# Turning the attention weights: from TensorE transposes to VectorE blocks and 16 transfers, with a new order of loads and conversions

## The chip, the cores and the metric

The kernel runs on one core of a Trainium2 chip. The metric is device time in microseconds (us), the median of several executions. A ratio in this text is the mean time of one kernel's fast runs over the mean time of the other kernel's fast runs of the same rounds, so it is not quite the ratio of the medians that are quoted.

Engine names in the profile: PE is TensorE, PEld its weight loads, DVE is VectorE, ACT is ScalarE, POOL is GpSimd, SPq is the DMA queue that SyncE issues. SBUF and PSUM are the core's two on-chip memories: in this kernel TensorE's results land in PSUM, and q, k, v and the weights e stand in SBUF. The granted clock is the share of full clock that TensorE got, by the profile's records. Each fp32 product of this kernel leaves two records on PE (x8 for the four products of a unit's scores), a transpose one; the counts below are of records.

## The reference

Eight batch rows go through attention with a threshold and then through a token and channel mixer; all is float32.

```python
# q, k, v: (8 rows, 8 heads, 576 queries/keys, 64)
scores = q @ k.T / 8
scores = where(scores >= max(scores) - tau, scores, -1e9)
attn   = exp(scores - max) / (sum + 1e-9)
x      = (attn @ v), heads side by side            # (8, 576, 512)
h  = relu(x.T @ w_tok1) @ w_tok2 ;  u = x + h.T    # 256 hidden tokens
out = u + relu(u @ w_ch1) @ w_ch2                  # 1536 hidden channels
```

The weights of the mixer arrive as float64 and are converted on the chip, in 31 pieces.

## The kernel before

A **unit** is 128 queries of a pair of heads; there are 18 units in a row, 144 in all. `t` is the unit's place (0 to 8) in a group of two pairs. While row b's attention runs, the mixer of row b-1 is cut into small steps, which `fill` puts between the attention's instructions. Row 0 has nothing to fill with.

```python
def load_pair(n, eng=nc.sync):        # 14 transfers a pair
    ...                               # lq, lk: 10 transfers in blocks of 32 columns
    vl = vlast[n % VL]
    for h in range(2):
        nc.sync.dma_start(out=lv[:, h], in_=v[b, 2*p+h, 0:MAIN, :]...)
        nc.sync.dma_start(out=vl[D*h:D*h+D, D*h:D*h+D], in_=v[b, 2*p+h, MAIN:S, :])   # v's last 64 rows

def scores(u):      # TensorE: q k^T into two PSUM tiles sc; then, for each head:
    nc.vector.tensor_reduce(out=mx..., in_=sc..., op=ALU.max)
    nc.gpsimd.tensor_scalar(out=bias..., in0=mx..., ...)
def weigh(u):       # ScalarE: e from sc (frees sc), then exp with the row sum
    nc.scalar.activation(out=eh, in_=sc[h]..., func=AF.Prelu, bias=bias...)
    nc.scalar.activation(out=eh, in_=eh, func=AF.Exp, ...)
def norm(u):        # VectorE 1/sum, GpSimd e *= 1/sum
def turn(u, third): # three 128x128 TensorE transposes into PSUM, then a copy to eT
    for c in range(3):
        nc.tensor.transpose(out=ps[:, c, :], in_=e[:, k0:k0+P], identity=ident)
    on = nc.scalar.copy if third == 1 else nc.vector.tensor_copy
    on(out=eT[...], in_=ps)
def values(...):    # TensorE: v^T eT, then a ScalarE copy to xT

for u in range(len(units) + LAG + 1):
    w = u - LAG
    if back and b_now: turn(w, 0); turn(w, 1)
    scores(u); norm(u - 1)
    for i in range(2 if b_now else 0, 3): turn(w, i)
    fill(0.4); weigh(u); fill(0.3)
    ...values of the units turned one step ago...
    fill(0.3)                          # in row 0 instead: weight(2), two steps of a conversion
    if t == 1: load_pair(n + 2)
    if t == 4: load_pair(n + 3)
    ...                                # t == 2, 7: VectorE turns the next q and k
```

Of the kernel before, what the change touches and what calls it, by code (L numbers as in the profile page):

```python
# [17 lines left out]
P = 128  # L18
# [3 lines left out]
def kernel(  # L22
# [11 lines left out]
):  # L34

# [53 lines left out]
    def load_pair(n, eng=nc.sync):  # L89


        b, p = pairs[n]
        lq = ld.tile([P, S // 32, 32], F32, tag="lq", name=f"lq_{n}")
        lk = ld.tile([P, S // 32, 32], F32, tag="lk", name=f"lk_{n}")
        lv = ld.tile([P, 2, NI, D], F32, tag="lv", bufs=4, name=f"lv_{n}")
        nl = LAST // 32
        for h in range(2):
            for c in range(2):
                r = slice(64 * h + 32 * c, 64 * h + 32 * c + 32)
                cols = slice(32 * c, 32 * c + 32)  # L100
                sq = q[b, 2 * p + h, :, cols].rearrange("(n t) d -> t n d", t=32)
                sk = k[b, 2 * p + h, :, cols].rearrange("(n t) d -> t n d", t=32)
                eng.dma_start(out=lq[r], in_=sq)
                if h == 0:
                    eng.dma_start(out=lk[r], in_=sk)
                else:
                    eng.dma_start(out=lk[r, nl:], in_=sk[:, : MAIN // 32])
                    eng.dma_start(out=lk[r, :nl], in_=sk[:, MAIN // 32 :])
        vl = vlast[n % VL]
        for h in range(2):  # L110
            nc.sync.dma_start(out=lv[:, h], in_=v[b, 2 * p + h, 0:MAIN, :].rearrange("(c p) d -> p c d", p=P))
            nc.sync.dma_start(out=vl[D * h : D * h + D, D * h : D * h + D], in_=v[b, 2 * p + h, MAIN:S, :])
        loaded[n] = (lq, lk, lv, vl)

    ident = const.tile([P, P], F32, name="ident")
# [3 lines left out]
    load_pair(0)  # L119
    load_pair(1, nc.scalar)  # L120
# [14 lines left out]
    abs_at = scratch[:, 2 * WMAX * NRAW + 2 * WMAX : 2 * WMAX * NRAW + 3 * WMAX].bitcast(F32)  # L135
# [7 lines left out]
    def f64_to_f32(dst, raw, rows, n):  # L143
# [10 lines left out]
        h = abs_at[0:rows, 0:n]  # L154
        turn_of[0] += 1
        af = a.bitcast(F32)
        nc.scalar.activation(out=lo.bitcast(I32), in_=lo, func=AF.Copy, scale=2.0**-29)
        yield nc.vector.tensor_scalar(
            out=a, in0=hi, scalar1=3, scalar2=0x3FFFFFFF, op0=ALU.logical_shift_left, op1=ALU.bitwise_and
        )  # L160
        nc.scalar.activation(out=h, in_=hi.bitcast(F32), func=AF.Abs)
# [3 lines left out]
        nc.vector.scalar_tensor_tensor(out=af, in0=h, scalar=2.0**-15, in1=af, op0=ALU.is_ge, op1=ALU.mult)  # L165
# [31 lines left out]
    def weight_ops():  # L197
        for i, (dst, src) in enumerate(pieces):
            raw, rows, n = raws.pop(i)
            if src.dtype == I64:  # L200
                for _ in f64_to_f32(dst, raw.bitcast(U32).rearrange("p (n w) -> p n w", w=2), rows, n):
                    yield
            else:
                nc.gpsimd.tensor_copy(out=dst, in_=like(raw, dst))
# [5 lines left out]
    done = 0  # L210

    def weight(n):

        nonlocal done
        for _ in range(n):
            if next(wops, wops) is wops:
                return
            done += 1

    for i in range(NRAW):  # L220
        load_piece(i)

# [9 lines left out]
    good = const.tile([P, 1], F32, name="good")  # L232
    ntau = const.tile([P, 1], F32, name="ntau")
    toff = const.tile([P, 1], F32, name="toff")
    tlow = const.tile([P, 1], F32, name="tlow")
    nc.vector.tensor_scalar(out=good, in0=tau_sb, scalar1=0.0, scalar2=None, op0=ALU.is_ge)
    nc.vector.tensor_scalar(out=tlow, in0=good, scalar1=1.0, scalar2=3.0e38, op0=ALU.subtract, op1=ALU.mult)
    nc.vector.tensor_scalar(out=ntau, in0=tau_sb, scalar1=0.0, scalar2=FAR, op0=ALU.max, op1=ALU.min)
    nc.vector.tensor_scalar(out=toff, in0=ntau, scalar1=-1.0 / SCALE, scalar2=None, op0=ALU.mult)
# [300 lines left out]
```

## Time and profile before

| | before |
|---|---|
| median | 1547.4 us (1547.0 to 1550.2; three runs. With a fourth, taken beside the changed kernel, 1547.2 us) |
| TensorE busy, share of the chain that ended last | 1472.7 us, 86% |
| mean granted TensorE clock | 0.99 |
| rows 0 and 1, from first scores to first scores | 101 and 188 us |
| rows 3 to 6, the same | 171, 187, 174, 190 us |

The busy share alone says little, since records of pipelined products overlap. The chain that ended last says more: where it runs through TensorE, only less work on TensorE shortens the kernel. Waits name who released whom. Few waits of TensorE over 1 us stand in the trace before (21, 40 us in all); the longest are at the start and in rows 0 and 1. The two kinds of wait that matter below are small here (who waited for whom; us in total, times, longest):

```profile
PE sc L271 <- ACT e L286: 6.8, 5, 2.0
...
PE c L393 <- ACT g L394: 2.8, 8, 0.7
```

### The profile page before, as it was taken

To read this page: it belongs to the slowest core of one execution; us is meant where nothing else is said; L and a number is where in the kernel's file an instruction comes from. 1 tells how busy PE (TensorE), PEld (TensorE's weight loads), DVE (VectorE), ACT (ScalarE), POOL (GpSimd) and SP (SyncE) were. 2 spreads that over 40 slices of the span, in tenths; PEclk is the share of its full clock that TensorE was granted. 3 is DMA by queue.
4 is the path that set the end of the run, shared out by engine and by line. 5 is a ranking of instruction groups with operands and counts; after the bars stand their busy time and mean duration, and the time that the engine had idled before them with its cause. 6 is when DMAs were issued, how large, how long until landed. Compare 5 with 4: busy or idle time off the path is not lost.

```text
span 1545.4 us, 20795 instructions
## 1 busy us (share of the span) xinstructions
PE 1472.7 (95%) x8000; PEld 951.0 (62%) x8000; DVE 542.4 (35%) x1127; ACT 674.3 (44%) x1463; POOL 335.7 (22%) x617
## 2 busy tenths in 40 slices
PE   5778799999999999999999999999999989999999
PEld 3444566647576567565756576566667556765665
DVE  4676763334333333323323342333322333201000
ACT  4776554445455344454434354444434444510110
POOL 2553542222222112212112222221111222200000
PEclk9998999999999999999999999999999999999999
DMA  6253413021111100200210201110201100000000
GB/s 115 68 113 91 132 56 60 8 53 24 31 31 31 31 14 18 47 14 7 54 35 3 43 19 31 31 31 1 60 8 31 31 8 7 1 14 7 7 14 21
DMA packets 206179, 54.05 MB, mean 35 GB/s; under 512 B 192704, under 2 KB 198848, under 8 KB 206080
## 3 DMA queue, kind: packets, MB, share of 16 engines
q1 hardware_dynamic: 201168, 52.13, 15.3%
q10 hardware_dynamic: 4912, 0.59, 0.4%
q8 instruction: 63, 1.03, 0.3%
q14 instruction: 36, 0.29, 0.1%
HBM read 43.25 MB, written 9.44 MB: 34 GB/s over the span
## 4 chain that ended last, share of the span: by engine, by line
PE 86%; ACT 6%; DVE 3%; DMA 2%; SPq 1%; POOL 1%; issue 1%; ACTq 0%; DVEq 0%
PE c L408 24%; PE c L393 22%; PE sc L271 10%; PE tr L321 10%; PE pv L338 7%; PE t L366 5%; PE t L372 3%; PE pv L335 3%; ACT e L289 2%; ACT e L286 2%; PE c L404 1%; PE tx L357 1%; DVE mx L276 1%; DMA lk<-in_k_dram 1%; ACT g L394 0%
## 5 line engine op out<-in xcount | busy, mean ns | idle before, releaser
L393 PE MATMUL c<-xT,wc 128*128 128x256 f32 (+1 forms) x1920 | 403.5, 362 | 4.3 <-ACT g L394 2.8
L408 PE MATMUL c<-wc,g 128*128 128x512 f32 x864 | 387.2, 593 | 0.0
L393 PEld LDWEIGHTS c<-xT,wc 128*128 128x128 f32 x1920 | 333.5, 191 | 59.9 <-ACT g L394 12.5
L323 DVE COPY eT<-tr 128x384 f32<-128x384 f32 x256 | 138.8, 546 | 437.3 <-PE tr L321 437.3
L277 POOL TENSOR_SCALAR bias<-mx,toff 128x1 f32<-128x1 f32 x288 | 76.7, 267 | 954.6 <-DVE mx L276 898.2
L408 PEld LDWEIGHTS c<-wc,g 128*128 128x128 f32 x864 | 157.5, 190 | 165.4 <-issue 164.3
L276 DVE TENSOR_REDUCE mx<-sc 128x1 f32<-128x576 f32 x288 | 204.6, 751 | 143.3 <-PE sc L271 143.2
L394 ACT ACTIVATE g<-c 128x256 f32<-128x256 f32 (+1 forms) x240 | 85.2, 363 | 383.8 <-PE c L393 383.8
L286 ACT ACTIVATE e<-sc,bias 128x576 f32<-128x576 f32 x288 | 199.1, 740 | 112.2 <-POOL bias L277 112.2
L289 ACT ACTIVATE e<-e,ntau,good 128x576 f32<-128x576 f32 x288 | 246.7, 864 | 0.0
L321 PE MATMUL tr<-ident,e 128*128 128x128 f32 x1296 | 210.0, 287 | 32.3 <-ACT eT L323 11.7
L321 PEld LDWEIGHTS tr<-ident,e 128*128 128x128 f32 x1296 | 146.2, 143 | 139.0 <-issue 90.8
L299 POOL TENSOR_SCALAR e<-e,rr 128x576 f32<-128x576 f32 x288 | 218.2, 770 | 19.0 <-DVE rr L296 3.6
L271 PE MATMUL sc<-kT,qT 64*128 64x288 f32 (+1 forms) x1280 | 193.1, 443 | 20.1 <-DVE kT L254 12.9
L271 PEld LDWEIGHTS sc<-kT,qT 64*128 64x128 f32 (+1 forms) x1280 | 103.6, 182 | 68.0 <-issue 20.3
L338 PE MATMUL pv<-eT,lv 128*64 128x256 f32 x1024 | 123.7, 384 | 0.0
L323 ACT COPY eT<-tr 128x384 f32<-128x384 f32 x128 | 61.1, 478 | 137.0 <-PE tr L321 136.7
L413 DVE COPY o<-c 128x512 f32<-128x512 f32 x36 | 24.9, 692 | 214.6 <-PE c L408 214.6
L338 PEld LDWEIGHTS pv<-eT,lv 128*64 128x64 f32 x1024 | 74.9, 139 | 38.6 <-issue 2.6
L372 PE MATMUL t<-w,a 128*128 128x288 f32 x256 | 73.1, 413 | 3.1 <-DVE xT L376 3.1
L366 PE MATMUL t<-x,w 128*128 128x512 f32 (+1 forms) x160 | 75.5, 610 | 0.0
L343 ACT COPY xT<-pv 128x256 f32<-128x256 f32 (+1 forms) x96 | 29.6, 320 | 102.2 <-PE pv L338 102.2
(43 smaller groups left out, 657.5 us busy)
## 6 DMA issues: line engine op xcount, KB each, us to landing
scratch<-in_moe_w_ch_dram SPq DMA_DIRECT2D x24, 512.0 KB, 3.6
out_dram<-o SPq DMA_DIRECT2D x36, 256.0 KB, 2.1
lq<-in_q_dram SPq DMA_DIRECT2D x124, 72.0 KB, 2.6
lv<-in_v_dram SPq DMA_DIRECT2D x64, 128.0 KB, 2.4
lk<-in_k_dram SPq DMA_DIRECT2D x62, 72.0 KB, 2.7
lk<-in_k_dram SPq DMA_DIRECT2D x62, 64.0 KB, 2.4
scratch<-in_moe_w_tok_dram SPq DMA_DIRECT2D x4, 288.0 KB, 3.0
vl<-in_v_dram SPq DMA_DIRECT2D x64, 16.0 KB, 2.1
```

The costliest lines, as they stand in the source:

```text
L271: nc.tensor.matmul(sc[h][rows, f, 0:HS], lhsT=qT[r, cols], rhs=kT[r, HS * f : HS * f + HS], start=True, stop=True)
L276: nc.vector.tensor_reduce(out=mx[:, c], in_=sc[h][:, :, 0:HS], axis=AX.XY, op=ALU.max)
L286: nc.scalar.activation(out=eh, in_=sc[h][:, :, 0:HS], func=AF.Prelu, bias=bias[:, h : h + 1], scale=SCALE, alpha=STEEP)
L289: nc.scalar.activation(out=eh, in_=eh, func=AF.Exp, bias=ntau, scale=good, accum_out=rs[:, h : h + 1])
L299: nc.gpsimd.tensor_scalar(out=eh, in0=eh, scalar1=rr[:, h : h + 1], scalar2=1.0, op0=ALU.mult, op1=ALU.mult)
L321: nc.tensor.transpose(out=ps[:, c, :], in_=e[:, k0 : k0 + P], identity=ident)
L323: on(out=eT[:, 3 * third : 3 * third + 3, c0 : c0 + P], in_=ps)
L338: nc.tensor.matmul(ps[D * h : D * h + D, 0:N], lhsT=lv[:, h, c, :], rhs=eT[:, (NI + 1) * h + c, cols], start=False, stop=(c == NI - 1), sk ...
L366: nc.tensor.matmul(ps, lhsT=w1[0:M, t, P * m : P * m + P], rhs=s["x"][0:M, t, :], start=(t == 0), stop=(t == NT - 1))
L372: nc.tensor.matmul(ps, lhsT=s["a"][:, m, P * c : P * c + P], rhs=w2[:, m, HS * f : HS * f + HS], start=(m == 0), stop=(m == NTK - 1))
L393: nc.tensor.matmul(ps, lhsT=wc1[:, j, c, :], rhs=uT[:, c, GR * i : GR * i + n], start=(c == 0), stop=(c == NCC - 1))
L408: nc.tensor.matmul(flat, lhsT=s["g"][:, j, P * t : P * t + P], rhs=wc2[:, j, :], start=False, stop=(j == NJ - 1), skip_group_check=True)
```

## The change

Its intent: take the transposes of e off TensorE, the bound engine. From row 1 on, VectorE turns e in 32x32 blocks inside SBUF, and 16 transfers per two units move the blocks to where a full transpose would have them. Keys are kept in natural order, so q and k need 8 loads and v one. The 64 rows of v that stand in two tiles are copied to `vl` by GpSimd. Conversions go at a steady pace.

```diff
-    def load_pair(n, eng=nc.sync):
+    def load_qk(n):                   # 8 transfers
+    def load_v(n):
+        lv = ld.tile([P, NK, D], F32, tag="lv", bufs=4, name=f"lv_{n}")
+        nc.sync.dma_start(out=lv, in_=v[b]...)
         vl = vlast[n % VL]
         for h in range(2):
-            nc.sync.dma_start(out=lv[:, h], in_=...)
-            nc.sync.dma_start(out=vl[D * h : D * h + D, D * h : D * h + D], in_=...)
+            r = slice(D * h, D * h + D)
+            nc.gpsimd.tensor_copy(out=vl[r, r], in_=lv[r, NI, :])
 ...
+    def turn_blocks(u):
+        key, place, n = group_of(u)
+        e = st.pop(u)
+        T = Ts[key][:, 0 : NK * n * P]
+        nc.vector.transpose(out=T.rearrange(...)[:, :, :, place, :], in_=e.rearrange("p (c a x) -> p c a x", c=NK, a=4))
+        if place == n - 1:
+            w = NK * n * 32
+            for a in range(4):
+                for i in range(4):
+                    nc.sync.dma_start(out=eTs[key][32*a : 32*a+32, w*i : w*i+w], in_=T[32*i : 32*i+32, w*a : w*a+w])
 ... (conversion: |hi| on ScalarE becomes hi*hi on GpSimd)
-        if back and b_now:
-            turn(w, 0)
-            turn(w, 1)
         if on:
             scores(u)
 ...
+            if in_blocks(key[0]):
+                turn_blocks(w)        # its products with v come two units later
+            else:
+                for i in range(3):
+                    turn(w, i)
 ...
+        weight(1 if b_now == 0 else 3)    # and weight(2) ahead of weigh(u)
         if on:
             if t == 1 and n + 2 < len(pairs):
-                load_pair(n + 2)
+                load_qk(n + 2)
+                load_v(n + 2)
```

More of the change, by code (lines that the diff above doesn't have):

```diff
@@ L87 @@
     vlast = [const.tile([P, P], F32, name=f"vl{i}") for i in range(VL)]
-    def load_pair(n, eng=nc.sync):
+    def load_qk(n):
         b, p = pairs[n]
-        lq = ld.tile([P, S // 32, 32], F32, tag="lq", name=f"lq_{n}")
-        lk = ld.tile([P, S // 32, 32], F32, tag="lk", name=f"lk_{n}")
-        lv = ld.tile([P, 2, NI, D], F32, tag="lv", bufs=4, name=f"lv_{n}")
-        nl = LAST // 32
-        for h in range(2):
-            for c in range(2):
-                r = slice(64 * h + 32 * c, 64 * h + 32 * c + 32)
-                cols = slice(32 * c, 32 * c + 32)
-                sq = q[b, 2 * p + h, :, cols].rearrange("(n t) d -> t n d", t=32)
-                sk = k[b, 2 * p + h, :, cols].rearrange("(n t) d -> t n d", t=32)
-                eng.dma_start(out=lq[r], in_=sq)
-                if h == 0:
-                    eng.dma_start(out=lk[r], in_=sk)
-                else:
-                    eng.dma_start(out=lk[r, nl:], in_=sk[:, : MAIN // 32])
-                    eng.dma_start(out=lk[r, :nl], in_=sk[:, MAIN // 32 :])
+        tiles = []
+        for src, tag in ((q, "lq"), (k, "lk")):
+            t = ld.tile([P, S // 32, 32], F32, tag=tag, name=f"{tag}_{n}")
+            for h in range(2):
+                for c in range(2):
+                    r = slice(64 * h + 32 * c, 64 * h + 32 * c + 32)
+                    nc.sync.dma_start(
+                        out=t[r], in_=src[b, 2 * p + h, :, 32 * c : 32 * c + 32].rearrange("(n t) d -> t n d", t=32)
+                    )
+            tiles.append(t)
+        loaded[n] = tiles
+    def load_v(n):
+        b, p = pairs[n]
+        lv = ld.tile([P, NK, D], F32, tag="lv", bufs=4, name=f"lv_{n}")
+        nc.sync.dma_start(out=lv, in_=v[b].rearrange("h s d -> (h s) d")[2 * S * p : 2 * S * p + 2 * S, :].rearrange("(c p) d -> p c d", p=P))
         vl = vlast[n % VL]
         for h in range(2):
-            nc.sync.dma_start(out=lv[:, h], in_=v[b, 2 * p + h, 0:MAIN, :].rearrange("(c p) d -> p c d", p=P))
-            nc.sync.dma_start(out=vl[D * h : D * h + D, D * h : D * h + D], in_=v[b, 2 * p + h, MAIN:S, :])
-        loaded[n] = (lq, lk, lv, vl)
+            r = slice(D * h, D * h + D)
+            nc.gpsimd.tensor_copy(out=vl[r, r], in_=lv[r, NI, :])
+        vals[n] = lv, vl
+    vals = {}
     ident = const.tile([P, P], F32, name="ident")
@@ L118 @@
         nc.gpsimd.memset(t, 0.0)
-    load_pair(0)
-    load_pair(1, nc.scalar)
+    load_qk(0)
     w1 = const.tile([P, NT, DTOK], F32, name="w1")
@@ L134 @@
     a_at = [scratch[:, 2 * WMAX * NRAW + WMAX * i : 2 * WMAX * NRAW + WMAX * (i + 1)] for i in range(2)]
-    abs_at = scratch[:, 2 * WMAX * NRAW + 2 * WMAX : 2 * WMAX * NRAW + 3 * WMAX].bitcast(F32)
+    sq_at = scratch[:, 2 * WMAX * NRAW + 2 * WMAX : 2 * WMAX * NRAW + 3 * WMAX].bitcast(F32)
     turn_of = [0]
@@ L153, in f64_to_f32 @@
         a = a_at[turn_of[0] % 2][0:rows, 0:n]
-        h = abs_at[0:rows, 0:n]
+        h2 = sq_at[0:rows, 0:n]
         turn_of[0] += 1
@@ L157, in f64_to_f32 @@
         nc.scalar.activation(out=lo.bitcast(I32), in_=lo, func=AF.Copy, scale=2.0**-29)
+        nc.gpsimd.tensor_tensor(out=h2, in0=hi.bitcast(F32), in1=hi.bitcast(F32), op=ALU.mult)
         yield nc.vector.tensor_scalar(
@@ L160, in f64_to_f32 @@
         )
-        nc.scalar.activation(out=h, in_=hi.bitcast(F32), func=AF.Abs)
         yield nc.vector.scalar_tensor_tensor(
@@ L164, in f64_to_f32 @@
         )
-        nc.vector.scalar_tensor_tensor(out=af, in0=h, scalar=2.0**-15, in1=af, op0=ALU.is_ge, op1=ALU.mult)
+        nc.vector.scalar_tensor_tensor(out=af, in0=h2, scalar=2.0**-30, in1=af, op0=ALU.is_ge, op1=ALU.mult)
         nc.gpsimd.tensor_tensor(
@@ L203, in weight_ops @@
             else:
+                yield
+                yield
                 nc.gpsimd.tensor_copy(out=dst, in_=like(raw, dst))
@@ L209 @@
     wops = weight_ops()
-    done = 0
+    steps_done = 0
     def weight(n):
-        nonlocal done
+        nonlocal steps_done
         for _ in range(n):
@@ L217, in weight, with need @@
                 return
-            done += 1
-    for i in range(NRAW):
+            steps_done += 1
+    def need(i):
+        weight(3 * i + 3 - steps_done)
+    load_piece(0)
+    load_qk(1)
+    load_v(0)
+    for i in range(1, NRAW):
         load_piece(i)
+    load_v(1)
     FAR = 104.0
     STEEP = 3.0e38
-    good = const.tile([P, 1], F32, name="good")
+    tlow = const.tile([P, 1], F32, name="tlow")
+    toff = const.tile([P, 1], F32, name="toff")
     ntau = const.tile([P, 1], F32, name="ntau")
-    toff = const.tile([P, 1], F32, name="toff")
-    tlow = const.tile([P, 1], F32, name="tlow")
-    nc.vector.tensor_scalar(out=good, in0=tau_sb, scalar1=0.0, scalar2=None, op0=ALU.is_ge)
-    nc.vector.tensor_scalar(out=tlow, in0=good, scalar1=1.0, scalar2=3.0e38, op0=ALU.subtract, op1=ALU.mult)
-    nc.vector.tensor_scalar(out=ntau, in0=tau_sb, scalar1=0.0, scalar2=FAR, op0=ALU.max, op1=ALU.min)
-    nc.vector.tensor_scalar(out=toff, in0=ntau, scalar1=-1.0 / SCALE, scalar2=None, op0=ALU.mult)
+    nc.vector.tensor_scalar(out=tlow, in0=tau_sb, scalar1=0.0, scalar2=-3.0e38, op0=ALU.is_lt, op1=ALU.mult)
+    nc.vector.tensor_scalar(out=toff, in0=tau_sb, scalar1=0.0, scalar2=FAR, op0=ALU.max, op1=ALU.min)
+    nc.vector.tensor_scalar(out=toff, in0=toff, scalar1=-1.0 / SCALE, scalar2=None, op0=ALU.mult)
     nc.vector.tensor_add(out=toff, in0=toff, in1=tlow)
-    nc.vector.tensor_scalar(out=ntau, in0=ntau, scalar1=-1.0, scalar2=None, op0=ALU.mult)
+    nc.vector.tensor_scalar(out=ntau, in0=toff, scalar1=SCALE, scalar2=None, op0=ALU.mult)
     heads = {}
@@ L247, with in_blocks @@
     eTs = {}
+    Ts = {}
+    def in_blocks(b):
+        return b > 0
     def prep(n):
-        lq, lk, lv, vl = loaded.pop(n)
+        lq, lk = loaded.pop(n)
         made = []
@@ L255, in prep @@
             made.append(sb)
-        heads[n] = made + [lv, vl]
+        heads[n] = made
     def scores(u):
@@ L267, in scores @@
             for n, cols, rows in parts:
-                qT, kT = heads[n][:2]
+                qT, kT = heads[n]
                 for h in range(2):
@@ L282, in weigh @@
         rs = small.tile([P, 2], F32, tag="rs", name=f"rs_{u}")
-        e = work.tile([P, 2 * S], F32, tag="e", bufs=4, name=f"e_{u}")
+        e = work.tile([P, 2 * S], F32, tag="e", bufs=3, name=f"e_{u}")
         for h in range(2):
@@ L288, in weigh @@
             eh = e[:, S * h : S * h + S]
-            nc.scalar.activation(out=eh, in_=eh, func=AF.Exp, bias=ntau, scale=good, accum_out=rs[:, h : h + 1])
+            nc.scalar.activation(out=eh, in_=eh, func=AF.Exp, bias=ntau, accum_out=rs[:, h : h + 1])
         st[u] = e, rs
@@ L300, in norm, with group_of @@
         st[u] = e
+    def group_of(u):
+        b, p0, t = units[u]
+        if t == SHARED:
+            return (b, p0, "s"), 0, 1
+        i, c = divmod(t - (t > SHARED), NI)
+        return (b, p0 + i, c // 2), c % 2, 2
     def turn(u, third):
-        b, p0, t = units[u]
+        key, place, n = group_of(u)
         e = st[u]
-        if t == SHARED:
-            key, c0 = (b, p0, "s"), 0
-        else:
-            i, c = divmod(t - (t > SHARED), NI)
-            key, c0 = (b, p0 + i, c // 2), P * (c % 2)
-        if third == 0 and c0 == 0:
-            if t == SHARED:
-                eTs[key] = work.tile([P, NK, P], F32, tag="eTs", bufs=1, name=f"eTs_{u}")
-            else:
-                eTs[key] = work.tile([P, NK, 2 * P], F32, tag="eT", name=f"eT_{u}")
+        if third == 0 and place == 0:
+            eTs[key] = work.tile([P, NK * 2 * P], F32, tag="eT", name=f"eT_{u}")
         if third == 2:
             st.pop(u)
-        eT = eTs[key]
+        eT = eTs[key][:, 0 : NK * n * P].rearrange("p (c x) -> p c x", c=NK)
         ps = ps_tr.tile([P, MAIN], F32, tag="tr", name=f"tr{third}_{u}")[:, 0 : 3 * P].rearrange("p (c x) -> p c x", c=3)
@@ L322, in turn @@
         on = nc.scalar.copy if third == 1 else nc.vector.tensor_copy
-        on(out=eT[:, 3 * third : 3 * third + 3, c0 : c0 + P], in_=ps)
-    def values(b, p, eT, cols, tok):
-        n = b * NP + p
-        lv, vl = heads[n][2:]
+        on(out=eT[:, 3 * third : 3 * third + 3, P * place : P * place + P], in_=ps)
+    def turn_blocks(u):
+        key, place, n = group_of(u)
+        e = st.pop(u)
+        if place == 0:
+            Ts[key] = work.tile([P, NK * 2 * P], F32, tag="T", name=f"T_{u}")
+        T = Ts[key][:, 0 : NK * n * P]
+        nc.vector.transpose(
+            out=T.rearrange("p (a c n x) -> p c a n x", a=4, c=NK, n=n)[:, :, :, place, :],
+            in_=e.rearrange("p (c a x) -> p c a x", c=NK, a=4),
+        )
+        if place == n - 1:
+            del Ts[key]
+            eTs[key] = work.tile([P, NK * 2 * P], F32, tag="eT", name=f"eT_{u}")
+            w = NK * n * 32
+            for a in range(4):
+                for i in range(4):
+                    nc.sync.dma_start(
+                        out=eTs[key][32 * a : 32 * a + 32, w * i : w * i + w], in_=T[32 * i : 32 * i + 32, w * a : w * a + w]
+                    )
@@ L329, in values @@
+    def values(b, p, c):
+        lv, vl = vals[b * NP + p]
         if b not in xTs:
             xTs[b] = xTs[b + 1] = work.tile([P, NP, 2 * S], F32, tag="xT", name=f"xT_{b}")
-        N = cols.stop - cols.start
-        ps = ps_tr.tile([P, MAIN], F32, tag="tr", name=f"pv_{n}_{tok}")
+        key = (b, p - p % 2, c) if c == "s" else (b, p, c)
+        n, N, tok = (1, LAST, MAIN) if c == "s" else (2, 2 * P, 2 * P * c)
+        first = LAST * (p % 2) if c == "s" else 0
+        eT = eTs[key] if c == "s" else eTs.pop(key)
+        if in_blocks(b):
+            eT = eT[:, 0 : NK * n * P].rearrange("p (i c x) -> p c i x", i=4, c=NK)
+            eT = eT[:, :, first // 32 : first // 32 + N // (32 * n), :]
+        else:
+            eT = eT[:, 0 : NK * n * P].rearrange("p (c x) -> p c x", c=NK)[:, :, first : first + N]
+        ps = ps_tr.tile([P, MAIN], F32, tag="tr", name=f"pv_{b}_{p}_{c}")[:, 0:N]
+        to = ps.rearrange("p (i x) -> p i x", x=32 * n) if in_blocks(b) else ps
@@ L333, in values @@
         for h in range(2):
             r = slice(D * h, D * h + D)
-            nc.tensor.matmul(ps[r, 0:N], lhsT=vl[:, r], rhs=eT[:, NI, cols], start=True, stop=False, skip_group_check=True)
+            nc.tensor.matmul(to[r], lhsT=vl[:, r], rhs=eT[:, NI], start=True, stop=False, skip_group_check=True)
         for c in range(NI):
             for h in range(2):
-                nc.tensor.matmul(
-                    ps[D * h : D * h + D, 0:N], lhsT=lv[:, h, c, :], rhs=eT[:, (NI + 1) * h + c, cols],
-                    start=False, stop=(c == NI - 1), skip_group_check=True,
-                )
@@ L342, in values @@
-        t0 = S * (b % 2) + tok
-        nc.scalar.copy(out=xTs[b][:, p, t0 : t0 + N], in_=ps[:, 0:N])
+                r = slice(D * h, D * h + D)
+                j = (NI + 1) * h + c
+                nc.tensor.matmul(to[r], lhsT=lv[:, j, :], rhs=eT[:, j], start=False, stop=(c == NI - 1), skip_group_check=True)
+        x = xTs[b][:, p, S * (b % 2) + tok : S * (b % 2) + tok + N]
+        if in_blocks(b) and n == 2:
+            x = x.rearrange("p (n i x) -> p i n x", n=n, x=32)
+            ps = ps.rearrange("p (i n x) -> p i n x", n=n, x=32)
@@ L346, in token_mlp @@
+        nc.scalar.copy(out=x, in_=ps)
     def token_mlp(b):
@@ L360, in tok1 @@
         def tok1(m):
+            need(2)
             if m == 0:
@@ L369, in tok2 @@
         def tok2(c, f):
+            need(6)
             ps = ps_mm.tile([P, HS], F32, tag="mm", name=f"t2_{b}_{c}_{f}")
@@ L388, in ch1 @@
         def ch1(j):
+            need(7 + j)
             if j == 0:
@@ L396, in ch2 @@
         def ch2(t, part):
+            need(7 + NJ + 3 * part + 2)
             t0 = GR * i + P * t
@@ L434, in fill @@
             step()
-            if b_now <= 1:
-                weight(2)
         if not todo:
@@ L452 @@
     prep(0)
-    due = []
+    due = deque()
     b_now = 0
     LAG = 2
-    for u in range(len(units) + LAG + 1):
+    for u in range(len(units) + LAG + 4):
         on = u < len(units)
@@ L462 @@
         back = 0 <= w < len(units)
-        ready, due = due, []
-        if back and b_now:
-            turn(w, 0)
-            turn(w, 1)
         if on:
@@ L471 @@
         if back:
-            for i in range(2 if b_now else 0, 3):
-                turn(w, i)
+            key, place, many = group_of(w)
+            if in_blocks(key[0]):
+                turn_blocks(w)
+            else:
+                for i in range(3):
+                    turn(w, i)
+            if place == many - 1:
+                b, p, c = key
+                when = u + (2 if in_blocks(b) else 1)
+                due += [(when, b, p + i, c) for i in range(2 if c == "s" else 1)]
         if b_now:
             fill(0.4)
+        weight(2)
         if on:
@@ L479 @@
             fill(0.3)
-        if back:
-            b, pq, tq = units[w]
-            if tq == SHARED:
-                due += [(b, pq + i, "s") for i in range(2)]
-            else:
-                i, c = divmod(tq - (tq > SHARED), NI)
-                if c % 2 == 1:
-                    due.append((b, pq + i, c // 2))
-        for b, p, c in ready:
-            if c == "s":
-                i = p % 2
-                values(b, p, eTs[b, p - i, c], slice(64 * i, 64 * i + 64), MAIN)
-            else:
-                values(b, p, eTs.pop((b, p, c)), slice(0, 2 * P), 2 * P * c)
-                if c == 1 and p == NP - 1:
-                    push(b)
+        while due and due[0][0] <= u:
+            _, b, p, c = due.popleft()
+            values(b, p, c)
+            if p == NP - 1 and c == 1:
+                push(b)
         if b_now:
             fill(0.3)
-        else:
-            weight(2)
+        weight(1 if b_now == 0 else 3)
         if on:
             if t == 1 and n + 2 < len(pairs):
-                load_pair(n + 2)
+                load_qk(n + 2)
+                load_v(n + 2)
             if t == 2:
@@ L505 @@
             if t == 4 and n + 3 < len(pairs):
-                load_pair(n + 3)
+                load_qk(n + 3)
+                load_v(n + 3)
             if t == 7 and n + 2 < len(pairs):
```

## The prediction

> **What bounds the kernel now.** I read the page first: engine shares, the slices and the chain that ended last.
>
> ```profile
> PE 1472.7 (95%) x8000; PEld 951.0 (62%) x8000; DVE 542.4 (35%) x1127; ACT 674.3 (44%) x1463; POOL 335.7 (22%) x617
> ...
> PE   5778799999999999999999999999999989999999
> ...
> PE 86%; ACT 6%; DVE 3%; DMA 2%; SPq 1%; POOL 1%; issue 1%; ACTq 0%; DVEq 0%
> PE c L408 24%; PE c L393 22%; PE sc L271 10%; PE tr L321 10%; PE pv L338 7%; PE t L366 5%; PE t L372 3%; PE pv L335 3%; ACT e L289 2%; ACT e L286 2%; PE c L404 1%; PE tx L357 1%; DVE mx L276 1%; DMA lk<-in_k_dram 1%; ACT g L394 0%
> ```
>
> TensorE bounds it. From slice 8 on (about 300 us) it stands at 9 in nearly every slice, and it carries 86% of the chain. Only the first 7 slices, 270 us, have slack: row 0 (no MLP to fill with) and row 1 (weights still converting). The part that the change attacks is "PE tr L321", 10% of the chain: the transposes of e.
>
> Second, the groups (line, engine, operation, tiles, shape, count, busy us and mean ns, idle before) for what each operation costs.
>
> ```profile
> L321 PE MATMUL tr<-ident,e 128*128 128x128 f32 x1296 | 210.0, 287 | 32.3 <-ACT eT L323 11.7 <-ACT xT L343 7.1 <-ACT eTs L323 5.2
> L323 DVE COPY eT<-tr 128x384 f32<-128x384 f32 x256 | 138.8, 546 | 437.3 <-PE tr L321 437.3
> L254 DVE STREAM_TRANSPOSE qT<-lq 128x576 f32<-128x576 f32 x32 | 24.6, 769 | 6.1 <-DMA lk<-in_k_dram 6.1
> ```
>
> Third, the timeline of a steady unit, since 287 ns is a modelled record with pipelining in it; starts are what count.
>
> ```profile
> 606.14 0.82 PE L321 MATMUL tr<-ident,e 128*128 128x128 f32 x6
> ...
> 606.89 1.24 PE L271 MATMUL sc<-kT,qT 64*128 64x288 f32 x8
> ...
> 608.06 0.55 PE L321 MATMUL tr<-ident,e 128*128 128x128 f32 x3
> 608.23 1.42 DVE L276 TENSOR_REDUCE mx<-sc 128x1 f32<-128x576 f32 x2 [1.00 <-PE sc L271]
> ...
> 608.45 0.81 PE L393 MATMUL c<-xT,wc 128*128 128x256 f32 x3
> ```
>
> Six transposes occupy TensorE from 606.14 to 606.89 (0.75 us) and three from 608.06 to 608.45 (0.39 us): 1.14 us per unit of 128 queries. Check: 10% of 1545 us over 144 units is 1.07 us.
>
> Fourth, the timeline of the DMA issues on the SyncE queue, because the change adds many.
>
> ```profile
> 1101.36 0.42 SPq L103 DMA_DIRECT2D lq<-in_q_dram  x1
> 1101.83 0.58 SPq L105 DMA_DIRECT2D lk<-in_k_dram  x1
> ...
> 1102.45 0.50 SPq L103 DMA_DIRECT2D lq<-in_q_dram  x1
> 1102.99 0.50 SPq L105 DMA_DIRECT2D lk<-in_k_dram  x1
> ```
>
> Back to back, one issue takes 0.54 us of that queue (1102.45 to 1102.99), whatever its size: the 16 KB loads of vl in the same stretch come at the same pace.
>
> **What the Trainium skill says.** (1) "VectorE: DVE Perf Modes", The three transpose paths: VectorE's transpose does independent 32x32 blocks into SBUF, TensorE's a full 128x128 into PSUM, so the latter needs an evacuation. The trace agrees: 144x3 evacuations (line 323) stand beside the transposes. (2) "TensorE: Matmul & The Clock Gate", Engine queue depths (under Part 1): VectorE, ScalarE and GpSimd are strict FIFO; only TensorE can pull weight loads ahead. The trace's order on these engines is the program's; one instruction that waits holds up all behind it. (3) "DMA: Bandwidth & Descriptors", Issuing engines are not separate DMA queues: the sequencer's time to start a DMA "is usually small relative to the DMA itself". Here it is not: a packet of 2304 B in this trace took 93 ns (median), a transfer of 32 rows is two packets on each of 16 DMA engines, so 0.2 us of engine time against 0.54 us of issue.
>
> **The change part by part.**
>
> *Transposes off TensorE.* Rows 1 to 7 are 126 units: 126 x 1.14 = 144 us of TensorE, all on the path. With them go their waits: between 302 and 1400 us TensorE waited 9 us for PSUM slots of tr (ScalarE's xT and x copies, VectorE's eT copies). Together -153.
>
> *VectorE.* It loses two evacuations per unit (2 x 0.546 = 1.09 us) and gains one 128x1152 block transpose. 576 columns take 0.77 us, of which about 0.6 are columns at 0.96 GHz, so 1152 take an estimated 1.35 us. Net +0.3 us per unit of some 8.5; VectorE is at about a third. Hidden. ScalarE loses 0.48 us per unit: hidden too.
>
> *16 transfers per group.* A row has 8 groups of two units and 2 of one: 160 transfers x 0.54 = 86 us of SyncE, plus 36 loads (19 us) and some 5 outputs: about 110 us of a row that will last about 150. Each of the 16 DMA engines gets two packets of a transfer: 320 a row, 30 us at 93 ns. So neither SyncE nor the DMA engines become the bound. The product with v comes two units later (before: one): its transfers are issued by 13 us after the unit's start and it is asked for at about 2.7 x 8.5 = 23 us. Hidden.
>
> *Fewer loads, but v's last 64 rows now pass through GpSimd.* Before, vl was filled by DMA. Now two GpSimd copies fill it from lv, standing in GpSimd's order right behind the load's place in the program and ahead of the next unit's bias. GpSimd will wait there for the load to land. At the unit where t = 1, SyncE has 16 transfers first. From that unit's scores: maxima done 2.8 us (608.23 + 1.42 - 606.89), rr 0.3, block transpose 1.35, so transfers start at 4.5; 16 x 0.54 to 13.1; 8 loads of q and k to 17.4; lv lands 2.4 later (its median) at 19.8; copies 0.3, bias 0.3, the prelu that frees the score PSUM 1.4: 21.8. TensorE wants that PSUM for the second next unit's scores at 2 x 8.5 = 17.0. That is a stall of nearly 5 us. It happens twice a row in rows 2 to 7 and once in row 1, without the last (no load): 12 x 5 = **+60**. At t = 4 no transfers stand ahead, and the load lands about 1 us inside the slack (prelu ends 612.0, next scores 615.5).
>
> *Rows 0 and 1.* Row 0 (13 to 114 us) is a chain of scores, maximum, bias, prelu; it has no transfers, but the four v loads behind 8 loads (about 7 us to landing against 2.2 us to the next bias) cost about 3 us each; a whole piece per unit instead of two thirds loads VectorE and GpSimd more; the first q and k arrive some 3 us sooner. I put +10. Row 1 lasts 188 us, row 3 with the same two MLP groups 171 (starts of their first scores): conversions came in bursts inside the fill. Pacing them returns about 20, so -20.
>
> Sum: 1547 - 153 - 20 + 10 + 60 = 1444 us; the tail (1400 to 1545 us, TensorE 142 us busy) is unchanged.
>
> **The rivals.**
> (a) The stall behind v's copies does not happen, because SyncE issues these transfers faster than loads or the slack is longer. For it: no transfer of 32 rows is in this trace. Against: all issues, large and small, come 0.47 to 0.6 us apart. Then about 1380.
> (b) SyncE or the DMA engines become the bound: transfers within SBUF land slowly, or the 0.54 grows to 0.9; then 160 x 0.9 + 24 fill a row of 168 us and the stall at t = 1 grows by 6 us. For it: 32 rows reach only a part of SBUF's DMA side. Against: 0.2 us of engine time each. Then 1500 to 1540.
> (c) VectorE's scattered write in runs of 32 is much slower than 1.35 us: the transfers start later and (b)'s stall grows by the same amount. Against: the qT transposes read and write plainly, so nothing speaks for it either way. At double, +1.35 x 12 = 16.
> (d) ScalarE is held up with bias, so the relu copies behind it also stop TensorE: the stall at t = 1 is then 8 us, not 5; 1480.
>
> **Range and chances.** The saving of 153 is nearly certain: it is TensorE's own time in stretches where it is 99% busy. The stall is the uncertain term, 0 to 110 us; rows 0 and 1 are worth 20 either way. I give the stall three chances in four. Predicted 1442 us, range 1375 to 1488; faster by over 2% 0.93, within 2% 0.05, slower 0.02.
>
> **What would show it.** Groups: line 321 has 162 transposes left; block transposes x126 at about 1.35 us. TensorE's busy time falls by some 140 us. Waits: GpSimd's vl copies waiting for DMA lv, about 24 waits, up to 10 us each; scores waiting for ScalarE's prelu at every t = 2 to 3 step, 60 us in all. SyncE timeline: bursts of 16 then 9 at 0.54. Wrong would be: scores that never wait (a), v products that wait for transfers (b), or row 0 longer by over 25 us.

## The result

The changed kernel takes **1624.9 us** (1622.2 to 1628.3), against 1547.2 us for the kernel before. The ratio is 1.050, with a 95% interval from 1.047 to 1.053. It is slower by 5% where I had predicted 7% faster.

The page of the changed kernel: busy time of each engine, the busy tenths of TensorE and its granted clock in 40 slices, and the chain by engine and by line.

```profile
PE 1397.5 (86%) x6866; PEld 860.7 (53%) x6866; DVE 582.8 (36%) x1000; ACT 574.7 (35%) x1306; POOL 376.3 (23%) x712
...
PE   3676689886979797979989797989989799999999
...
PEclk9867799997989898999999899998999899999999
...
PE 63%; SPq 14%; DVE 6%; issue 5%; DMA 4%; ACT 4%; POOL 3%; POOLq 0%; DVEq 0%
PE c L461 19%; PE c L445 19%; PE sc L288 10%; SPq L360 9%; SPq L103 5%; PE pv L387 4%; DMA lv<-in_v_dram 4%; PE t L416 4%; PE t L423 3%; DVE mx L293 2%; ACT e L303 2%; DVE T L350 2%; PE pv L382 2%; ACT e L306 1%; PE tx L406 1%
```

TensorE's busy time did fall, though by 75 us and not 140. But its row of slices, solid from slice 8 on before, now dips regularly. The dips repeat twice a row, and after many of them the clock dips too. The chain leaves TensorE for 37% of the time and runs through VectorE's block turn (line 350), the transfers (360), the loads of q and k (103) and the landing of v ("DMA lv").

The waits of the changed kernel (who waited for whom; us in total, times, longest):

```profile
POOL vl L117 <- DMA lv<-in_v_dram: 374.3, 30, 19.2
...
PE sc L288 <- ACT e L303: 129.3, 25, 18.1
...
PE c L445 <- ACT g L446: 39.4, 7, 10.0
```

GpSimd stood 374 us before its copies into `vl` until v had landed. TensorE waited 129 us for score PSUM and 39 us for relu copies.

One such place in row 5, from the scores of the unit with t = 1 on (timeline: start us, duration us, engine, line, operation, tiles, count, and in brackets the idle time before it with its releaser):

```profile
893.19 1.24 PE L288 MATMUL sc<-kT,qT 64*128 64x288 f32 x8
...
896.08 1.36 DVE L350 STREAM_TRANSPOSE T<-e 128x1152 f32<-128x1152 f32 x1
...
897.50 11.12 SPq L360 DMA_DIRECT2D eT<-T  x16
...
903.98 1.24 PE L288 MATMUL sc<-kT,qT 64*128 64x288 f32 x8
...
905.15 5.45 PE L445 MATMUL c<-xT,wc 128*128 128x256 f32 x24
905.25 1.42 DVE L293 TENSOR_REDUCE mx<-sc 128x1 f32<-128x576 f32 x2 [7.81 <-PE sc L288]
...
908.66 2.26 SPq L103 DMA_DIRECT2D lq<-in_q_dram  x4
...
910.97 2.12 SPq L103 DMA_DIRECT2D lk<-in_k_dram  x4
913.18 0.44 SPq L113 DMA_DIRECT2D lv<-in_v_dram  x1
916.42 0.52 POOL L117 COPY vl<-lv 64x64 f32<-64x64 f32 x2 [18.60 <-DMA lv<-in_v_dram]
917.04 0.50 POOL L294 TENSOR_SCALAR bias<-mx,toff 128x1 f32<-128x1 f32 x2
917.34 1.37 ACT L303 ACTIVATE e<-sc,bias 128x576 f32<-128x576 f32 x2 [9.78 <-POOL bias L294]
...
920.12 0.65 ACT L446 ACTIVATE g<-c 128x256 f32<-128x256 f32 x2
920.54 3.78 PE L445 MATMUL c<-xT,wc 128*128 128x256 f32 x8 [9.95 <-ACT g L446]
924.25 2.25 PE L288 MATMUL sc<-kT,qT 64*128 64x288 f32 x8
```

This is the sequence to learn. The maxima of the unit that began at 903.98 were done at 906.7. Their two bias instructions take 0.5 us and could have run then. But the copies into `vl` stand ahead of them in GpSimd's order, and they wait for a load that SyncE could issue only at 913.18, behind 16 transfers and 8 loads. So bias comes at 917.04, ScalarE's prelu at 917.34, the relu copies behind it at 920.12, and TensorE stands from 910.6 to 920.5. At the end, the four score products (x8) take 2.25 us and not 1.24: the clock had dropped to half, for 13.7 us by the trace's clock records.

To add this up over the whole trace I took the gap between the starts of successive products, less the time in which the first of them streams (0.84 ns a column; 24 dense records of 512 columns take 10.3 us). Gaps over 1 us are counted as waits, and the streaming time added at half clock is counted apart.

| | before | after |
|---|---|---|
| streaming at full clock, us | 1336 | 1215 |
| waits over 1 us, us (number) | 40 (21) | 198 (32) |
| slower streaming at half clock, us | 9 | 43 |
| time at half clock by the clock records, us | 31 | 225 |

The 121 us of streaming saved are the transposes: 1134 of 128 columns at 0.107 us. That is more than the 75 us by which busy time fell: the longer streaming at half clock (34 us more) is most of the difference. Waits cost 158 us more and the clock 34 us more. The sum of the three, +71 us, leaves 4 us of the +75 us between the two traces (1545.4 and 1620.4 us) to the start and to gaps under 1 us.

### The profile page after: what moved, and what is told of

It reads as the page before. It is cut to its first block, busy times and chain, and to the rows that moved or that the text cites. A ratio compares the mean times of both kernels' runs of the same rounds, so it can differ in the third digit from the quotient of the medians.

```text
span 1620.4 us, 19436 instructions
## 1 busy us (share of the span) xinstructions
PE 1397.5 (86%) x6866; PEld 860.7 (53%) x6866; DVE 582.8 (36%) x1000; ACT 574.7 (35%) x1306; POOL 376.3 (23%) x712
## 4 chain that ended last, share of the span: by engine, by line
PE 63%; SPq 14%; DVE 6%; issue 5%; DMA 4%; ACT 4%; POOL 3%; POOLq 0%; DVEq 0%
PE c L461 19%; PE c L445 19%; PE sc L288 10%; SPq L360 9%; SPq L103 5%; PE pv L387 4%; DMA lv<-in_v_dram 4%; PE t L416 4%; PE t L423 3%; DVE mx L293 2%; ACT e L303 2%; DVE T L350 2%; PE pv L382 2%; ACT e L306 1%; PE tx L406 1%
## 5 line engine op out<-in xcount | busy, mean ns | idle before, releaser
L445 PE MATMUL c<-xT,wc 128*128 128x256 f32 (+1 forms) x1920 | 416.1, 369 | 40.6 <-ACT g L446 39.4
L461 PE MATMUL c<-wc,g 128*128 128x512 f32 x864 | 397.1, 606 | 0.0
L288 PE MATMUL sc<-kT,qT 64*128 64x288 f32 (+1 forms) x1280 | 220.5, 466 | 137.1 <-ACT e L303 129.3
L288 PEld LDWEIGHTS sc<-kT,qT 64*128 64x128 f32 (+1 forms) x1280 | 121.9, 193 | 226.7 <-ACT e L303 150.4
L306 ACT ACTIVATE e<-e,ntau 128x576 f32<-128x576 f32 x288 | 220.1, 772 | 0.0
L350 DVE STREAM_TRANSPOSE T<-e 128x1152 f32<-128x1152 f32 x126 | 172.5, 1369 | 16.7 <-DMA eT<-T 10.4
L117 POOL COPY vl<-lv 64x64 f32<-64x64 f32 x64 | 14.8, 232 | 395.2 <-DMA lv<-in_v_dram 374.3
L423 PEld LDWEIGHTS t<-w,a 128*128 128x128 f32 x256 | 46.3, 194 | 36.3 <-DVE xT L427 15.1
L427 DVE TENSOR_TENSOR xT<-xT,t 128x288 f32<-128x288 f32 x64 | 27.9, 441 | 97.5 <-PE t L423 97.4
L392 ACT COPY xT<-pv 128x256 f32<-128x256 f32 x64 | 23.8, 372 | 102.3 <-PE pv L387 102.2
```

The lines of the kernel that those rows point to most:

```text
L288: nc.tensor.matmul(sc[h][rows, f, 0:HS], lhsT=qT[r, cols], rhs=kT[r, HS * f : HS * f + HS], start=True, stop=True)
L306: nc.scalar.activation(out=eh, in_=eh, func=AF.Exp, bias=ntau, accum_out=rs[:, h : h + 1])
L350: nc.vector.transpose(out=T.rearrange("p (a c n x) -> p c a n x", a=4, c=NK, n=n)[:, :, :, place, :], in_=e.rearrange("p (c a x) -> p c a ...
L423: nc.tensor.matmul(ps, lhsT=s["a"][:, m, P * c : P * c + P], rhs=w2[:, m, HS * f : HS * f + HS], start=(m == 0), stop=(m == NTK - 1))
L445: nc.tensor.matmul(ps, lhsT=wc1[:, j, c, :], rhs=uT[:, c, GR * i : GR * i + n], start=(c == 0), stop=(c == NCC - 1))
L461: nc.tensor.matmul(flat, lhsT=s["g"][:, j, P * t : P * t + P], rhs=wc2[:, j, :], start=False, stop=(j == NJ - 1), skip_group_check=True)
```

## The experiments

Theory A: GpSimd's wait for v causes the loss. It waits in program order, holds up the next unit's bias, and the clock loss follows. Rival B: the transfers themselves are the cost, as queue time or as late products with v. Rival C: the paced conversions, now with a GpSimd multiply, lengthen row 0 (148 us against 101). Medians are in us; "before" in these rounds was 1547.8 to 1547.9.

### e1: vl by DMA again

```diff
-            nc.gpsimd.tensor_copy(out=vl[r, r], in_=lv[r, NI, :])
+            k0 = MAIN if h == 0 else 0
+            nc.sync.dma_start(out=vl[r, r], in_=v[b, 2 * p + h, k0 : k0 + LAST, :])
```

> The changed kernel, but vl is again filled by two small DMAs per pair and GpSimd copies nothing. Theory A (GpSimd waits in its order for the load of v, holds up the next unit's bias, and TensorE then also loses its clock): the 374 us of GpSimd waits and the 129 + 39 us of TensorE waits go, the granted clock returns to 0.99, row 0 to about 105 us; 1375 to 1395 us. Rival B (the 16 transfers per group on the SyncE queue are the cost): hardly any change, over 1580 us. Rival C (the paced conversions with squares on GpSimd cost row 0 its 47 us): about 1425 us, row 0 still 140 us or more.

Measured: 1432.5, ratio 0.926 to before. The clock is at 0.98 and row 0 takes 109 us. This undoes one line of the change, and 192 us go. Rivals B and C fall as the main cause: transfers and pacing are all still there. But it is 37 us above the upper end of the expected 1375 to 1395: the gains had been put too high as well (e5).

### e2: the same copies, later

```diff
-            nc.gpsimd.tensor_copy(...)              # in load_v
+            ...                                     # pairs 0 and 1 at unit 2
+            if t == 6 and n + 2 < len(pairs):
+                fill_vl(n + 2)                      # the two copies of a pair, 5 units after its load
+            if t == 8 and n + 3 < len(pairs):
+                fill_vl(n + 3)                      # 4 units after
```

> The changed kernel with the same two GpSimd copies per pair, but placed 4 to 5 units after the load (t = 6 and t = 8; for the first two pairs at unit 2), so that they find the data landed. Theory A: as e1 within 10 us, so 1370 to 1390 us; that tells the wait from the copies' own 15 us. If the copies themselves (port sharing, their 0.23 us) mattered, it would stay above 1450 us. Rival B: over 1580 us.

Measured: **1426.3**, ratio 0.921 to before; row 0 takes 109 us. It is within 10 us of e1, as theory A had it, but 36 us above the 1370 to 1390 given. The GpSimd copies are the same 64 instructions, so neither their own time nor the port sharing that the expectation allowed for is the cause. It is the wait: 199 us between the changed kernel and this one. The same place in this kernel's timeline:

```profile
755.97 1.24 PE L290 MATMUL sc<-kT,qT 64*128 64x288 f32 x8
...
760.28 11.01 SPq L362 DMA_DIRECT2D eT<-T  x16
...
766.75 1.24 PE L290 MATMUL sc<-kT,qT 64*128 64x288 f32 x8
...
767.93 7.51 PE L447 MATMUL c<-xT,wc 128*128 128x256 f32 x32
...
768.88 0.26 POOL L296 TENSOR_SCALAR bias<-mx,toff 128x1 f32<-128x1 f32 x1 [8.30 <-DVE mx L295]
...
775.36 1.00 PE L290 MATMUL sc<-kT,qT 64*128 64x288 f32 x6
...
775.86 0.44 SPq L113 DMA_DIRECT2D lv<-in_v_dram  x1
```

v is issued just as late (19.9 us after the scores, against 20.0 in the changed kernel), but bias runs 2.1 us after its scores, and TensorE goes from 768 to 775 without a gap.

### e3 and e4: transposes back on TensorE

```diff
     def in_blocks(b):
-        return b > 0
+        return False
```

e3 is this alone; e4 also has e2's late copies.

> The changed kernel with the block transposes and transfers undone: TensorE turns e in all rows; loads, key order, waiting copies and pacing stay. Theory A: GpSimd still waits for v, about 7 us each time and not 10 to 19, since no transfers stand ahead; row 0 as long as in the changed kernel (148 us), small stalls later: 1580 to 1620 us. Rival B: as the kernel before, 1530 to 1560 us, since the transfers are gone.

> Both undone: TensorE turns e in all rows and the copies come late; what is left of the change is fewer loads, natural key order and paced conversions. Theory A: row 0 about 100 us, row 1 some 15 to 20 us shorter than before: 1520 to 1535 us, and e2 is 145 to 155 us below it. Rival C: row 0 longer than before by 30 us or more: 1550 to 1580 us.

Measured: e3 1696.4, e4 1624.6. Both are far above what I expected, for a reason that was mine: I had undone the block turns, but not the order in which the kernel before mixed its transposes with the scores. The waits of e4 show it:

```profile
PE tr L341 <- ACT eT L343: 80.8, 142, 0.6
```

Nine transposes in a row need three PSUM slots and have two, and 142 units wait 0.57 us each for an evacuation. So e4 is no measure of "the rest of the change". The difference of the two is still useful. In this order of the transposes, with no transfers ahead of v, the waiting copies cost 72 us (e3 less e4). With block turns and transfers they cost 199 us (changed kernel less e2). Pacing and squares alone do not lengthen row 0 by 47 us either: it takes 107 us in e4.

### e5: transposes on TensorE in their old order, copies late

```diff
+        if back and b_now:
+            turn(w, 0)
+            turn(w, 1)
         if on:
             scores(u)
 ...
-                for i in range(3):
+                for i in range(2 if b_now else 0, 3):
```

> TensorE turns e in all rows, in the order of the kernel before (two thirds ahead of the scores, one behind), copies late. e4 had 81 us of TensorE waiting for ScalarE's evacuations, which I put down to the three thirds in a row on two PSUM slots. If so these waits fall to about 10 us and the run is at 1535 to 1550 us: then loads, key order and pacing are worth nothing in sum, and the block transposes are worth this run minus e2, 110 to 125 us, not the 153 that I predicted. Rival: the waits stay and another part of the change (lv in one load, eT's shared buffers) makes them: 1600 us or more.

Measured: 1538.3, ratio 0.994 (0.992 to 0.996). The evacuation waits are 9 us:

```profile
PE tr L341 <- ACT eT L343: 9.1, 16, 0.6
```

This is the control that e4 should have been. Fewer loads, key order and pacing are worth 9.5 us in sum; no run takes them apart. The block transposes are worth 1538.3 - 1426.3 = 112 us. The three parts, -9.5 - 112 + 198.6 = +77, give the measured change, but that is no check: each is the difference of two neighbouring kernels in one order of changes, and in another order the shares differ (72 and not 199 us for the waiting copies between e4 and e3).

### e6: loads ahead of the transfers, v first

```diff
         if on:
+            for at, m in ((1, n + 2), (4, n + 3)):
+                if t == at and m < len(pairs):
+                    load_v(m)
+                    load_qk(m)
             scores(u)
```

The copies stay where they were, at the unit's end.

> The changed kernel with the waiting copies left where they are, but the loads of v, q and k issued at the start of the unit, v first and ahead of the 16 transfers. Theory A (the length of GpSimd's wait is what stands ahead of v on the SyncE queue): v lands before the copies come up, waits of GpSimd for v under 40 us in all, 1425 to 1445 us as e2. Rival: a GpSimd copy of freshly loaded data waits anyway: over 1550 us.

Measured: 1433.2. GpSimd waits 68 us for v, more than the 40 I gave:

```profile
POOL vl L120 <- DMA lv<-in_v_dram: 67.9, 15, 12.7
```

This is without harm after the first unit, where the copies for pairs 0 and 1 still stand ahead of the first bias (10.7 us). The length of the harmful wait is thus set by what stands ahead of v on SyncE's queue.

### e9: only v first

```diff
-                load_qk(n + 2)
                 load_v(n + 2)
+                load_qk(n + 2)
```

(The same for n + 3.)

> The changed kernel with one swap: of the nine loads of a pair, v goes first and no longer last, still behind the 16 transfers and with the copies where they were. Each wait of GpSimd for v gets 8 x 0.54 = 4.3 us shorter. Theory A (the waits turn into time about one to one once their slack is used up, and the clock adds a little): some 17 waits that stop TensorE, 73 us and about 10 us of clock, so 1535 to 1555 us. If only the longest part, the transfers, mattered: over 1600 us; if any wait at all were the trouble: over 1600 us too.

Measured: 1533.1, ratio 0.991 to before, 2 us under the range of theory A. GpSimd's waits for v fall from 374 us to 268:

```profile
POOL vl L117 <- DMA lv<-in_v_dram: 268.1, 32, 14.8
```

Swapping two lines takes 92 us off the changed kernel: TensorE's waits over 1 us fall from 198 to 118 us and the half-clock term from 43 to 36. Shortening the waits turns into time about one to one where TensorE stood, as theory A has it.

### e7: useless products in the wait

```diff
+        if on and b_now > 1 and t == 2 and n + 2 < len(pairs):
+            idle = ps_tr.tile([P, MAIN], F32, tag="tr", name=f"idle_{u}")
+            for i in range(8):
+                nc.tensor.matmul(idle, lhsT=ident, rhs=wc2[:, i, :], start=(i == 0), stop=(i == 7))
```

> The changed kernel with 8 useless 128x512 products (about 6.8 us of TensorE) put into each of the 11 long waits of rows 2 to 7 (unit t = 2); the result stays right, nobody reads them. Theory: the waits also halve TensorE's clock afterwards, by my count from the trace 24 us of slower streaming from row 2 on; with less idle time the clock stays: granted clock up from 0.93 to about 0.96, and 1600 to 1612 us although there is more work. Rival (the clock plays no part): 1622 to 1635 us.

Measured: 1626.7, against 1624.9: no gain, and inside the range of the rival. The clock did rise as expected, from 0.931 to 0.952, and half-clock time from row 2 on fell from 133 to 58 us. But the slower streaming there fell only from 24 to 15 us. The 75 us of added products took the place of 67 us of waits, so 8 us were lost where a wait was shorter than 6.8 us. So the time itself shows no share of the clock: that a gain of 9 us stands against a loss of 8 is a count on the trace too. The 34 us in the table above rest on counting alone, and what the clock is worth is not shown by any run here.

### e8: e2 with work kept for the start of row 2

```diff
-        quota = (sum(c for c, _ in todo) - (KEEP if b else 0.0)) / (UB - 1)
+        quota = (sum(c for c, _ in todo) - (KEEP if b else 20.0)) / (UB - 1)
```

> e2 with 20 us of row 0's MLP kept back for the first units of row 2, which in e2 have nothing to fill with (units of 6.5, 6.3 and 3.2 us, then products waiting 6 us for their transfers). Expected 1414 to 1421 us; if these short units were harmless, 1426 as e2.

Measured: **1414.1**, ratio 0.914 (0.912 to 0.915) to before, the best of all. In e2, row 0's mixer runs out before row 1's is ready. The first units of row 2 are then so short that products overtake their transfers:

```profile
301.00 1.90 PE L290 MATMUL sc<-kT,qT 64*128 64x288 f32 x8 [1.98 <-ACT e L305]
...
308.68 1.12 PE L384 MATMUL pv<-eT,vl 128*64 128x256 f32 x4 [5.78 <-DMA eT<-T]
```

Rows 1 and 2 together take 297 us in e8 and 313 in e2.

### All in one table

| run | what | us | waits over 1 us | slower streaming at half clock |
|---|---|---|---|---|
| before | | 1547.2 | 40 | 9 |
| after | the change | 1624.9 | 198 | 43 |
| e1 | vl by DMA | 1432.5 | 45 | 15 |
| e2 | copies late | 1426.3 | 44 | 14 |
| e3 | TensorE turns, copies wait | 1696.4 | 79 | 22 |
| e4 | TensorE turns, copies late | 1624.6 | 25 | 8 |
| e5 | as e4, old order of turns | 1538.3 | 33 | 8 |
| e6 | loads ahead of transfers | 1433.2 | 50 | 14 |
| e7 | products in the wait | 1626.7 | 134 | 36 |
| e8 | e2, work kept for row 2 | 1414.1 | 34 | 11 |
| e9 | v ahead of q and k | 1533.1 | 118 | 36 |

And by row (from the first scores of a row to those of the next, us):

| | start | row 0 | 1 | 2 | 3 | 4 | 5 | 6 | 7 and tail |
|---|---|---|---|---|---|---|---|---|---|
| before | 13 | 101 | 188 | 152 | 171 | 187 | 174 | 190 | 369 |
| e5 | 9 | 110 | 178 | 152 | 171 | 186 | 175 | 189 | 367 |
| after | 8 | 148 | 189 | 171 | 180 | 189 | 183 | 189 | 364 |
| e2 | 8 | 109 | 168 | 145 | 149 | 169 | 157 | 170 | 352 |
| e8 | 8 | 109 | 156 | 141 | 152 | 170 | 156 | 170 | 351 |

## Why the prediction was wrong

**The step that failed** is the term "12 x 5 = **+60**", the stall of TensorE behind v's copies, with the "+10" for row 0 beside it. The mechanism was named rightly: the instruction that waits, the load it waits for, the transfers ahead of it, the PSUM that TensorE then lacks, and the 12 places. Its size was wrong: the copies' waiting costs 199 us (after less e2). The prediction had put 72 us on it: the 60, and the four loads of 3 us inside row 0's +10. The missing 127 us turn 1442 into 1569 (the prediction's own terms add up to 1444); the remaining 56 us up to 1625 are gains that I had put too high (below). One of the signs that I had named for being wrong came true: row 0 is 47 us longer, where 25 was the limit. Four things made the term small:

1. Each estimate on the way to the copy was a little short. A transfer takes 0.633 us of the queue (median of the spacing) and not 0.54, so "whatever its size" was wrong: loads of q and k still take 0.54. The burst takes 10.1 us, not 8.6. v lands 3.2 us after its issue, not 2.4; one load now moves 288 KB, as the profile counts it, where one before moved 128. In row 5, bias was done 24.4 us after the scores of the unit at t = 1, and not the predicted 20.4. When the slack has been used up, 4 us more of wait are 4 us more of stall, nearly double.
2. Rival (d) came true beside the main stall: TensorE waited 39 us, 7 times, for relu copies. ScalarE also waits in order, so its relu copies stop behind the late prelu. Where the fill is of the first channel product, TensorE stands on "PE c <- ACT g" before it even comes to the scores. The 11 long waits from row 2 on average 9.5 us, where I had "nearly 5" and in rival (d) 8.
3. The clock was not in the sum at all. In and after its waits TensorE runs at half clock: 225 us in all, against 31 before. By counting this is 34 us.
4. Rows 0 and 1. I took 3 us for each of row 0's four loads of v; three of them cost 8.5 to 9.3 us and one 6.3. I overlooked a fifth: the copies for pairs 0 and 1 stand ahead of the very first bias (9.0 us). Row 0 pays 39 us and row 1 21 us (after less e2). The remaining 135 us of the two traces' difference lie in rows 2 to 7, where the prediction had 11 x 5 = 55.

**The other steps, in order.**

- *TensorE is the bound, and its transposes are on the path*: right. e5 less e2 is 112 us.
- *-153 for transposes and their waits*: right in kind, 37% too high. In rows 3 to 6 a row gains 19.4 us (e5 to e2), where I had 153/7 = 21.9. The chain's 1.07 us per unit, which I used only as a check, was nearer than the 1.14 of the timeline. Rows 1 and 2 gain only 9 and 7 us, since there the work between the products runs out (e8).
- *VectorE's block turn 1.35 us, hidden*: right; 1.369 us, 126 times. Rival (c) is out.
- *SyncE and the DMA engines do not become the bound; the products with v two units later find their data*: right in the full rows. Of TensorE's waits in e2 only 7.8 us are for transfers, at the start of row 2. Rival (b) is out as a bound, though the 93 ns of the prediction were too low: they are the median of few packets of 2304 B (512, on average 133 ns); in the changed kernel one took 144 ns on average, 162 ns in the median.
- *At t = 4 inside the slack*: right from row 2 on. Three short waits of 1.0 to 4.1 us stand there.
- *Row 1: -20 by pacing*: mostly wrong. In e5, rows 0 and 1 together end 6 us earlier than before: row 1 is 10 us shorter, row 0 8 us longer, and it begins 4 us sooner.

Taken apart, the prediction had -153 - 20 + 10 + 60. The runs gave -112 for the turns, -9.5 for the rest and +199 for the copies.

What stays open: the clock's own share. Counting gives 34 us of the 199. e7, meant to test it, filled 67 us of waits and did not get faster, so the share is argued and not shown. Open too is how the 9.5 us divide between fewer loads, key order and pacing.

## What to carry to other kernels

Before an instruction goes onto an in-order engine right behind the issue of a load, look at what else that engine owes, and at what stands ahead of the load on its queue. Here 64 copies of 0.23 us, put right behind their loads, cost 199 us, and 4 to 5 units later in the program the same copies did not. When many small transfers are added to a queue, every later load of that queue becomes later by the whole burst, so put the loads first, or use the data later. And when an experiment undoes half of a change, check that it has restored the old order as well as the old operations.

## What the Trainium skill lacked or had wrong

- "DMA: Bandwidth & Descriptors", Issuing engines are not separate DMA queues, calls the sequencer's time to start a DMA "usually small relative to the DMA itself". For transfers of 32 rows of 2304 B within SBUF, issue took 0.633 us each. Their 32 packets, if shared evenly by the 16 DMA engines, are about 0.29 us of each (an estimate, 2 x 144 ns), so issue set the pace, though a single transfer landed only 2.0 us after its issue. A burst of 16 held the queue for 10.1 us.
- "TensorE: Matmul & The Clock Gate", Engine queue depths, says that ScalarE, VectorE and GpSimd are strict FIFO, and the traces agree. No page read here draws the consequence: a GpSimd copy of 232 ns behind a late load held back bias, prelu and relu copies, and TensorE for up to 18 us.
- The same page, Part 1, says that an idle window of about 3.4 us halves the clock. The traces agree in part: half-clock stretches last 3.4 us or multiples of it (up to 20.5 us), 225 us in all. But in 11 of the changed kernel's 23 drops before the work's end TensorE had by the gaps been idle for less than 3.4 us (2.3 us in row 5, at 912.7), so a whole idle window was not needed here. My prediction cited this page and did not use this part of it.
- The same page, Part 4, gives about 275 ns for a 128x128 transpose in a kernel's context. Here the records say 287 ns, but six fp32 transposes started within 0.75 us, and the chain charges 119 ns for each (10% of 1545 us over 1296).
- "VectorE: DVE Perf Modes", The three transpose paths, gives 311 ns for one 128x128 block turn in bf16. Here 128x1152 in fp32, written in scattered runs of 32, took 1369 ns, 152 ns for each 128x128.
